# Another fixed order list for a one-core transformer block: loads, evacuations and buffer slots placed anew

## The chip, the cores and the metric

The kernel runs on one core of a Trainium2 chip, in one launch. The metric is device time in microseconds, the median of several runs; lower is better. The core has five instruction queues that run beside each other, each in its own order: TensorE (PE, matrix products into PSUM), VectorE (DVE), ScalarE (ACT), GpSimd (POOL) and the sync queue (SP), which here only issues DMA transfers.

## The reference

One transformer block on x of 2048 tokens by 640, all tensors bf16: memory-augmented attention ("Infini-attention", 32 heads of 20, four segments of 512 tokens), then an MLP of width 1728 with SiLU.

```python
qs, ks, vs = (q[:, :, s].copy(), k[:, :, s].copy(), v[:, :, s].copy())     # s = 0..3
p = _softmax(einsum('bhqd,bhkd->bhqk', qs, ks) * scale + mask)             # causal in the segment
a_dot = einsum('bhqk,bhkd->bhqd', p, vs)
num = einsum('bhld,bhde->bhle', phi(qs), M)
den = einsum('bhld,bhd->bhl', phi(qs), z)[..., None] + 1e-06
o = g * num / den + (1.0 - g) * a_dot
M = M + einsum('bhld,bhle->bhde', phi(ks), vs);  z = z + phi(ks).sum(l)
...
h = x + attention(layernorm(x)) @ wo
out = h + silu(layernorm(h) @ w1) @ w2
```

phi(t) is t + 1 where t > 0 and exp(t) elsewhere.

## The kernel before

The 16 blocks of 128 tokens belong to four segments ("seg 0" to "seg 3") of four blocks. Each segment passes the same stages, and the work of neighbouring segments is interleaved:

- LayerNorm of each block (`n1_st`, `n1_ra`, `n1_rb`, `n1_ap`; lines 711 to 732): statistics on DVE, reciprocal root on POOL in two steps, scaling on DVE. The transposed copy xT is made for the first four blocks by TensorE (`n1_tp`, line 741) and an evacuation on ScalarE (`n1_te`, line 750), for later blocks by a DMA transpose (`n1_tr`, line 756).
- V for one block (`v00` is seg 0, block 0; line 783) with an evacuation (`ve`, lines 793 and 794), and ten projections per segment (`pr`, line 817: `pr` segment, group of heads, 0 for Q or 1 for K) with evacuations (`qe`, lines 825 and 826). Q and K use weights rearranged on chip from wq and wk (`re_`, lines 682 and 684).
- The features phi (`ex`, `pha`, `phb`), copies by DMA that move head parts to other partitions (`vt`, line 857).
- Scores by groups of four heads (`qk`, line 893), their exponentials on ScalarE (`e`, line 904), causal masks on POOL (`mk`, line 915), the product with V (`av`, line 936), its evacuation (`oe`, lines 949 and 951), the transposition and the memory term (`tn`, lines 965 and 969), the normalization on DVE (`nm`) and the sum on POOL (`ad`).
- The memory M (`kt`, `mz`, `ma`, `mb`; line 1058) for the next segment.
- The projection by wo (`ot`, `wo`, line 1119) with the residual (`rs`), a second LayerNorm (`n2_`), the MLP's first product (`h1`, lines 1148 and 1153) with tanh on ScalarE (`th`, line 1162) and a product on DVE into sT (`s`, line 1168), and the second product (`h2`, line 1195), the last residual (`o`, line 1208) and the store (`out`, line 1213).

Nothing is planned at run time or by a cost model. `ORDER` is a list of task names, written out in the kernel. A task is emitted when its name comes up, so the order on every engine's queue, the SP queue's DMAs included, is that of the list. After a name, `/A` or `/D` says whether ScalarE or DVE does an evacuation that both could do, and the numbers after a colon are the buffer slots (PSUM banks, score buffers and so on) that the task's new tiles take. `fill30:0` stands for 30 matmuls on zeros into PSUM bank 0 (line 604), whose result nobody reads. A tracker then adds a semaphore wait wherever an instruction reads what another engine or DMA wrote, or overwrites what another reads.

The loads of weights and of x (lines 567 and 570) are issued by SP, except x2 and x3, which ScalarE issues. `load_x(8, 4)` and `x4` bring four blocks each, `x0` to `x3` one. w1 has five parts by rows (`w_w1_0` to `w_w1_4`), w2 four (`w_w2_0` to `w_w2_3`) and two small ones. wq and wk land in the space of sT and are rearranged from there. `zf0` (ScalarE, line 633) and `zf1` (DVE, line 635) prepare a table from beta; the products `mzc` on POOL (line 657) read it, and `lsc0` to `lsc3` (lines 622 to 630) prepare the scales that `oe` reads. `mt`, `mta`, `mtb` and `mm` are constant masks made on POOL (lines 643 to 653).

Of the kernel before, what the change touches and what calls it, by code (L numbers as in the profile page):

```python
# [6 lines left out]
ALU = mybir.AluOpType  # L7
# [317 lines left out]
D = 640  # L325
# [33 lines left out]
zpad:0 vpad0 iota x3:4 x1:3 x0:7 x2:5 sel w_wv:0 warm:0 vpad1 w_q:0 w_k halfc epsc beta x4:0,1,2,6 n1_st0:1 w_wo:0  # L359
w_w2_4 n1_st1:6 n1_ra0 w_w1_0:0 n1_rb0 n1_ap0:0 n1_ra1 n1_st2:2 fill30:0 n1_tp0:4 n1_rb1 n1_te0/A:0 n1_st3:0 n1_ra2  # L360
epsg0 n1_rb2 fill8:1 v00:0 mt1 n1_ap2:1 n1_ra3 n1_ap1:0 n1_rb3 n1_tp1:2 n1_tp2:6 mt2 n1_ap3:2 n1_te1/A re_wq1/D:0
n1_tp3:4 n1_te2/A re_wq4/D v01:2 ve00/D:1 n1_te3/A re_wq2/A pr010:6 re_wk0/A:0 re_wk1/D ve01/D pr011:7 qe010/D:0
re_wk3/D re_wk4/A lsc0 lsc1 re_wq0/D pr001:0 re_wk2/D qe011/A qk1x0:4 qe001/D:0 pr000:1 e1x2:5 n1_st6:0 e1x0 pr021:0
re_wq3/D qe000/A n1_ra6 mk1x_0 lsc2 n1_st7:4 ex001:0 qk0x0:4 n1_rb6 pr020:2 e0x2:0 mt3 mk1x_256 qe021/D:0 e0x0 lsc3
pr041:3 n1_st5:5 qe020/A vt00:0 n1_st4:7 qk2x0:4 n1_ra5 qe041/A:0 mk0x_0 pr031:1 zf0 vt09 vt06 e2x2:2 n1_rb5 mk0x_256
pr030:0 e2x0 n1_ap5:2 pha041:1 x8:8,9,10,11 qe031/A:0 mk2x_0 vt03 qk0yb0:4 qe030/D av1x:3 e0yb0:1 pr040:2 mk2x_256
n1_ra7 pha001:0 e0yb2 oe1x/D:0 av0x:3 qe040/D mk0yb_0 qk1yb0:4 oe0x/A:1 av2x:0 e1yb0:3 tn1x:1 v03:2 pha021:2 nm1x:3,0
e1yb2 mk0yb_256 phb001 n1_ap6:1 oe2x/A:0 mk1yb_0 qk3x0:4 ve03/D v02:0 n1_tr5:0 vt011 vt07 e3x2:4 vt04 n1_rb7 n1_st9:1
e3x0 ex021:2 ve02/D vt05 vt010 qk4x0:4 mk3x_0 n1_ra4 tn0x:2 e4x0:6 nm0x:0 vt01 mk3x_256 e4x2 n1_st8:6 fill7:3 qk0ya0:0
mta1 vt02 av3x:4 e0ya0:5 mk4x_0 vt08 oe3x/D:1 n1_st10:0 mk4x_256 e0ya2 fill6:5 qk1ya0:4 n1_tr6 v11:0 n1_rb4 e1ya0:0  # L370
n1_st11:3 n1_ra10 mta3 kt00:1 n1_ra8 e1ya2 av4x:2 ve11/D:0 tn2x:3 n1_ra11 phb021 qk5x0:4 n1_ap4:3 fill10:0 v12:0 e5x2:2
n1_ap7:1 n1_tr4 oe4x/D:0 e5x0 nm2x:1 ex011:2 n1_tr7 ve12/D qk6x0:4 mk5x_0 tn4x:2 e6x0:4 av0y:3 nm4x:0 mk5x_256 tn3x:0
e6x2 oe0y/D:0 kt02:0 n1_rb11 av5x:1 ex041:1 n1_ap11:3 qk7x0:4 mk6x_0 v10:2 nm3x:1 w_w2_5 e7x2:6 oe5x/D:1 mta2 mtb3 e7x0
mk6x_256 w_w1_1 w_w1_4 ve10/D qk2ya0:4 mk7x_0 v13:0 e2ya2:5 n1_ra9 mk7x_256 mk1yb_256 e2ya0 tn0y:2 av7x:3 ve13/D n1_rb8
oe7x/A:0 qk2yb0:4 nm0y:1 tn7x:0 e2yb0:1 av6x:1 nm7x:2 tn5x:2 av1y:3 e2yb2 oe6x/D:1 nm5x:3 tn6x:0 oe1y/A:0 qk3ya0:4
mk2yb_0 nm6x:0 e3ya0:2 n1_rb10 ot1:0 mk2yb_256 pha011:0 phb011 e3ya2 tn1y:2 pr101:1 mz02:0 qe101/D:0 av2y:3 ot0 ma02/A:3
qk3yb0:4 oe2y/D:1 mz00:1 e3yb2:0 phb041 pr100:3 ma00/D:0 kt01:1 nm1y:1 e3yb0 tn2y:2 zf1 qe100/D qk4ya0:4 mk3yb_0 kt04:0
wo1:0 e4ya0:6 nm2y:2 mk3yb_256 mtb1 e4ya2 w_w2_2 av3y:3 rs1 w_w1_3 ex031:0 qk4yb0:4 oe3y/D:0 w_w1_2 wo0:0 e4yb2:5
n2_st1:5 w_w2_1 e4yb0 epsg1 tn3y:2 ex101:1 n2_ra1 rs0 mm5 qk5ya0:4 pr140:3 n2_rb1 mk4yb_0 n2_st0:2 e5ya2:0 e5ya0 pr121:0
n2_ap1:0 n2_ra0 nm3y:0 qe140/A:0 mt0 n2_rb0 n2_tr1:0 qk5yb0:4 pr141:1 mta0 e5yb2:3 n2_ap0:2 mk4yb_256 n2_tr0 e5yb0 mtb0  # L380
pha031:1 phb031 av4y:2 mm6 qk6ya0:4 mm4 qe121/D:0 ex140:2 mk5yb_0 pr111:3 e6ya2:6 mk5yb_256 e6ya0 pr120:0 qe111/D:0
qe141/D ex121:0 qk6yb0:4 pha101:2 av5y:3 e6yb0:4 oe4y/D:0 h1_0_7_0:1 qe120/D e6yb2 h1_0_0_0:2 oe5y/D:1 th0_7_0:1 mk6yb_0
mk6yb_256 qk7ya0:4 th0_0_0:0 s0_7_0:0 tn4y:0 h1_0_8_0:3 e7ya0:2 nm4y:3 mz01:1 s0_0_0 mz04:0 e7ya2 ma01/D:2 phb101 kt10:0
kt03:1 h1_0_3_0:2 ma04/D:1 tn5y:1 th0_8_0:1 qk7yb0:4 th0_3_0:0 s0_8_0 av6y:0 e7yb0:0 s0_3_0 h1_0_1_0:3 nm5y:1 e7yb2
h1_0_12_0:2 th0_1_0:1 mk7yb_0 qk8a0:4 th0_12_0:0 pr110:1 e8a2:1 s0_12_0 s0_1_0 mm0 mk7yb_256 e8a0 mzc0 h1_0_10_0:2
qe110/D av7y:3 th0_10_0:1 vt19:0 qk8e0:4 s0_10_0 pr130:1 e8e2:0 vt16 oe6y/D:1 w_w2_3 n1_ap10:2 oe7y/D:0 e8e0 h1_0_5_0:2
pha121:0 qe130/D:0 w_w2_0 h1_0_11_0:3 th0_5_0:1 mk8e_0 qk8b0:4 s0_5_0 th0_11_0:0 tn7y:0 h1_0_6_0:1 e8b0:6 nm7y:3 mz03:2
ma03/D:4 s0_11_0 e8b2 h1_0_2_0:0 pha100:0 n1_ap8:1 h1_0_13_0:2 pha120:0 th0_2_0:1 qk9a0:4 mk8b_0 th0_13_0:0 pr131:3
s0_13_0 e9a2:4 mk8a_0 s0_2_0 mk8b_384 e9a0 h1_0_4_0:0 qe131/D n1_tr8:0 mk8e_256 h1_0_9_0:2 pha141:2 th0_6_0:1 mm3
th0_4_0:0 qk9b0:4 s0_6_0 mzc4 mzc6 ex100:1 mk9a_0 vt17 av8:3 s0_4_0 th0_9_0:1 mzc3 pha110:0 e9b2:3 h2_0_0:0 mm2 phb100  # L390
phb121 s0_9_0 mm9 pha111:1 mtb2 vt18 vt110 mzc9 mm8 e9b0 mm11 h2_0_1 oe8/D:0 mzc5 n1_tr10 ex141:1 mk9b_0 mm10 qk10a0:4
tn6y:3 h2_0_2 e10a2:5 phb141 mm1 vt11 nm6y:0 mzc2 n1_rb9 h2_0_3 e10a0 vt13 mb01:0 mm7 vt111 mzc1 qk10b0:4 mk9b_384 o0
h2_1_0:2 e10b2:2 ot3 mb00:0 e10b0 tn8:0 h2_1_1 n1_tr11 ex120:0 mk10b_0 nm8:2,1 qk10e0:4 ex111:1 h2_1_2 vt15 mk10b_384
phb111 n1_ap9:0 e10e2:1 mk10a_0 vt14 av9:0 e10e0 phb120 ot2 h2_1_3 oe9/A:0 ex110:0 mk10e_0 mk10e_256 qk11a0:4 kt12:1 o1
# [66 lines left out]
def build(nc, es, A_x, A_wq, A_wk, A_wv, A_wo, A_beta, B_x, B_w1, B_w2, out):  # L461
# [52 lines left out]
    zpad = sb("zpad", [128, 256], BF16)  # L514
# [54 lines left out]
    def load_w(k, dst, src, prio, bw, wr, kind="plain", engs=(SP,)):  # L569
# [17 lines left out]
        reads=R((C, ["zpad"])), writes=R((W["w2"], [4, 5]))), [(C, ["zpad"])], [(W["w2"], [4, 5])], -100)  # L587
# [681 lines left out]
```

## Time and profile before

| What | Value |
|---|---|
| median of three runs | 304.64 us (304.49 to 305.93) |
| span of the profiled execution | 303.6 us |
| median less that span | 1.04 us |
| TensorE busy | 294.4 us, 97% |
| DVE, ScalarE, POOL busy | 214.4 (71%), 226.6 (75%), 141.7 us (47%) |
| read from HBM, written | 10.41 MB, 2.62 MB |
| first product with a weight (v00, line 783) starts | 9.03 us |

The profiled execution is known by its span, from the first to the last instruction; the time of a run holds about a microsecond more. PE in the profile is TensorE's matmuls, PEld its weight loads, which run beside them. A row of the timeline or of a group gives line, engine, operation, destination and source, the count, and after the count in brackets how long the engine was idle just before and what ended that. The chain follows the work that ended last backwards to what released it. SPq is the time that SP spends on issuing. In the rows by stage the columns are the window, its length, the busy time of PE, PEld, DVE, ACT and POOL with instruction counts, the granted TensorE clock as a share of full speed, the mean busy share of the 16 DMA engines, and GB/s moved. In the rows on DMA the last number is the median time in us from issue to landing.

### The profile page before, as it was taken

The page shows a single profiled execution, that of the slowest core. Times are in us where ns is not written, and L with a number is a line of the kernel's source. Part 1 is how long each engine was busy: PE and PEld are TensorE (multiplying, and loading weights), DVE is VectorE, ACT ScalarE, POOL GpSimd, SP SyncE. Part 2 cuts the span into 40 slices and gives each one's busy share as a digit, 9 for nine tenths or more (in the row PEclk, how much of TensorE's full clock was granted, in tenths as well). Part 3 has the DMA queues.
Part 4 walks back from the last instruction along what each step waited for, and adds up shares of the span by engine and source line. Part 5 has one row for each costly group of instructions (what it writes and reads, how often), then busy time and mean ns, then how long its engine had stood idle before and what let it go on. Part 6 is the DMA issues. An engine that isn't in the chain of part 4 may idle for free.

```text
span 303.6 us, 7334 instructions
## 1 busy us (share of the span) xinstructions
PE 294.4 (97%) x2934; PEld 167.9 (55%) x2934; DVE 214.4 (71%) x492; ACT 226.6 (75%) x321; POOL 141.7 (47%) x280
## 2 busy tenths in 40 slices
PE   6999989999999999999999999999999999999996
PEld 5634545466565455566643545556564466764565
DVE  4888967877868866958588975858847494835623
ACT  3689988999999999899889989968779951004500
POOL 3346574532875856546847317564564730400000
PEclk9999999999999999999999999999999999999999
DMA  6938375843544130063551300043241006221003
GB/s 211 363 104 159 69 153 87 272 37 77 166 87 75 39 42 2 2 122 69 106 154 42 67 19 0 2 89 69 56 97 36 2 0 89 43 66 66 0 3 107
DMA packets 48721, 24.65 MB, mean 81 GB/s; under 512 B 39152, under 2 KB 47600, under 8 KB 48688
## 3 DMA queue, kind: packets, MB, share of 16 engines
q1 hardware_dynamic: 48400, 23.86, 34.6%
q8 instruction: 23, 0.38, 0.5%
q10 hardware_dynamic: 288, 0.33, 0.4%
q14 instruction: 10, 0.08, 0.1%
HBM read 10.41 MB, written 2.62 MB: 43 GB/s over the span
## 4 chain that ended last, share of the span: by engine, by line
PE 72%; ACT 12%; DVE 7%; DMA 4%; SPq 2%; issue 1%; POOL 0%; ACTq 0%
PE ps_all L1195 17%; PE ps_all L1153 13%; PE ps_all L817 13%; ACT PT L904 8%; PE ps_all L893 7%; PE ps_all L1119 6%; PE ps_all L783 5%; PE ps_all L936 5%; DVE sT L1168 3%; DMA wv_sb<-in_A_wv_dram 2%; ACT th L1162 2%; PE ps_all L965 2%; PE ps_all L1058 2%; DMA x_tok<-in_A_x_dram 1%; PE ps_all L969 1%
## 5 line engine op out<-in xcount | busy, mean ns | idle before, releaser
L904 ACT ACTIVATE PT<-ps_all 128x1024 bf16<-128x1024 f32 (+1 forms) x168 | 156.3, 985 | 16.9 <-PE ps_all L893 15.9
L915 POOL TENSOR_SCALAR_AFFINE_SELECT PT<-PT 128x512 bf16<-128x512 bf16 x128 | 81.5, 650 | 52.8 <-ACT PT L904 51.5
L1195 PE MATMUL ps_all<-w_sb,sT 128*128 128x320 bf16 (+2 forms) x462 | 64.8, 295 | 0.1
L1153 PE MATMUL ps_all<-hT,w_sb 128*128 128x512 bf16 (+1 forms) x325 | 62.5, 337 | 0.5 <-DVE sT L1168 0.4
L1162 ACT ACTIVATE th<-ps_all 128x512 f32<-128x512 f32 (+2 forms) x70 | 34.0, 505 | 35.1 <-PE ps_all L1153 24.6
L1168 DVE SCALAR_TENSOR_TENSOR sT<-th,ps_all 128x512 bf16<-128x512 f32 (+2 forms) x70 | 37.6, 558 | 23.8 <-ACT th L1162 23.2
L1195 PEld LDWEIGHTS ps_all<-w_sb,sT 128*128 128x128 bf16 x462 | 43.2, 98 | 18.5 <-issue 1.9
L1153 PEld LDWEIGHTS ps_all<-hT,w_sb 128*128 128x128 bf16 x325 | 29.8, 98 | 25.4 <-issue 2.1
L1010 POOL TENSOR_TENSOR otok<-on 128x320 bf16<-128x320 bf16 x24 | 19.2, 804 | 23.7 <-DVE on L1002 23.6
L711 DVE BATCH_NORM_STATS2 stt<-x_tok 128x6 f32<-128x320 bf16 x64 | 27.8, 476 | 3.4 <-DMA x_tok<-in_A_x_dram 3.2
L1208 DVE SCALAR_TENSOR_TENSOR x_tok<-ps_all,x_tok 128x640 bf16<-128x640 f32 (+3 forms) x18 | 13.3, 748 | 19.0 <-PE ps_all L1195 18.9
L720 POOL TENSOR_TENSOR rst<-mvt,eps_c 128x1 f32<-128x1 f32 x32 | 7.1, 223 | 40.4 <-DVE mvt L714 36.0
L817 PE MATMUL ps_all<-xT,wqr 128*128 128x512 bf16 x100 | 25.0, 381 | 0.0
L783 PE MATMUL ps_all<-wv_sb,xT 128*128 128x320 bf16 x160 | 24.4, 300 | 0.4 <-DMA wv_sb<-in_A_wv_dram 0.3
L817 PE MATMUL ps_all<-xT,wkr 128*128 128x512 bf16 x100 | 24.8, 380 | 0.0
L1119 PE MATMUL ps_all<-wo_sb,oT 128*128 128x320 bf16 x160 | 24.1, 299 | 0.4 <-DVE rd L996 0.2
L936 PE MATMUL ps_all<-PT,Vx 128*32 128x256 bf16 (+3 forms) x576 | 24.4, 287 | 0.0
L893 PE MATMUL ps_all<-QK 20*128 20x256 bf16 (+3 forms) x360 | 20.5, 286 | 1.0 <-ACT PT L904 0.7
L1002 DVE TENSOR_TENSOR on<-ps_all,rd 128x640 bf16<-128x640 f32 x24 | 19.8, 824 | 1.9 <-POOL otok L1010 1.1
L826 DVE CAST QK<-ps_all 128x512 bf16<-128x512 f32 x25 | 16.9, 684 | 5.1 <-PE ps_all L817 5.0
L1119 PEld LDWEIGHTS ps_all<-wo_sb,oT 128*128 128x128 bf16 x160 | 14.8, 97 | 8.1 <-issue 2.8
L783 PEld LDWEIGHTS ps_all<-wv_sb,xT 128*128 128x128 bf16 x160 | 14.7, 98 | 7.9 <-issue 1.5
(71 smaller groups left out, 329.4 us busy)
## 6 DMA issues: line engine op xcount, KB each, us to landing
out_dram<-x_tok SPq DMA_DIRECT2D x15, 160.0 KB, 1.9
w_sb<-in_B_w_dram SPq DMA_DIRECT2D x5, 432.0 KB, 4.5
x_tok<-in_A_x_dram SPq DMA_DIRECT2D x3, 640.0 KB, 5.3
w_sb<-in_B_w_dram SPq DMA_DIRECT2D x3, 480.0 KB, 3.8
QKV<-QK SPq DMA_DIRECT2D x16, 72.0 KB
wv_sb<-in_A_wv_dram SPq DMA_DIRECT2D x1, 800.0 KB, 7.2
sT<-in_A_wq_dram SPq DMA_DIRECT2D x1, 800.0 KB, 8.9
sT<-in_A_wk_dram SPq DMA_DIRECT2D x1, 800.0 KB, 10.6
```

The lines of the kernel that those rows point to most:

```text
L711: T.add(DV, lambda e, hh=hh: e.bn_stats(out=stt[:, s, 6 * hh:6 * hh + 6], in_=xb[:, 320 * hh:320 * hh + 320]), reads=R((xa, xsub)), writes ...
L783: fns.append(lambda e, c=c, hh=hh: e.matmul(bank(ps, hh)[:, 0:320], lhsT=xT[:, c, 128 * i:128 * i + 128], rhs=wv_sb[:, c, 320 * hh:320 * h ...
L817: fns = [lambda e, kc=kc: e.matmul(bank(ps)[:, lo:hi], lhsT=wt[:, kc, c, :], rhs=xT[:, kc, lo:hi], start=(kc == 0), stop=(kc == NC - 1)) f ...
L893: fns.append(lambda e, j=j, o=o, r=r, q0=q0, q1=q1, qa=qa, ka=ka: e.matmul(ps_all[:, o:o + q1 - q0], lhsT=ka[32 * r:32 * r + DH, 128 * j:1 ...
L904: T.add(AC, lambda e: e.activation(out=pt[:, pta.slot, q0:q0 + 2, 0:width], in_=sc3[:, b0:b0 + 2, 0:width], func=ACT.Exp, scale=SCALE), re ...
L915: T.add(PO, lambda e: e.affine_select(out=v, in_=v, pattern=[[0, 4], [1, 128]], compare_op=ALU.is_ge, fill=0.0, base=0, channel_multiplier ...
L936: fns.append(lambda e, j=j, r=r, h=h, pa=pa, pt=pt, co=co, q0=q0, ji=ji: e.matmul(bank(po)[32 * r:32 * r + 32, q0:hi], lhsT=Vx[:, vx.slot, ...
L1119: fns.append(lambda e, c=c, hh=hh: e.matmul(bank(ps, hh)[:, 0:320], lhsT=oT[:, c, 128 * i:128 * i + 128], rhs=wo_sb[:, c, 320 * hh:320 * h ...
L1153: fns = [lambda e, c=c: e.matmul(bank(ps)[:, lo:hi], lhsT=w1_sb[:, c, 128 * f:128 * f + 128], rhs=hT[:, c, lo:hi], start=(c == 0), stop=(c ...
L1162: T.add(AC, lambda e: e.activation(out=th[:, tha.slot, lo:hi], in_=bank(ps)[:, lo:hi], func=ACT.Tanh, scale=0.5), reads=R((ps, [0])), writ ...
L1168: T.add(DV, lambda e: e.scalar_tensor_tensor(out=sT[:, f, lo:hi], in0=th[:, tha.slot, lo:hi], scalar=1.0, in1=bank(ps)[:, lo:hi], op0=ALU. ...
L1195: fns.append(lambda e, f=f, t0=t0, fr=fr, hh=hh, n=n: e.matmul(bank(pa, hh)[:, 0:n], lhsT=sT[:, f, t0:t0 + 128], rhs=w2_sb[:, fr, c0 + 320 ...
```

## The change

The list holds the same tasks in another order. The tasks' code is the same but for one line. The engine of some evacuations changes, as do most slots. The fillers were 30, 8, 7, 6 and 10 matmuls at five places; they are 44, 19 and 4 at three places, all ahead of the first product with a weight. All loads of the start change places: before, SP issues x1, x0, wv, wq, wk, beta, x4, wo; after, parts of w1 and w2, wo, x8 and beta stand first, wq is the eighth, x0 and x1 come behind it, and wk and wv further down (14th and 17th). The constants on POOL, before spread among the attention of seg 0 and later, stand near the top.

Beside the list, the product into sT is now declared to write two keys in segments 1 to 3, where it declared one; seg 0 has its own two halves as before. The tracker therefore lets these writes also wait for seg 0's readers of the second half.

```diff
 ORDER = """
-zpad:0 vpad0 iota x3:4 x1:3 x0:7 x2:5 sel w_wv:0 warm:0 vpad1 w_q:0 w_k halfc epsc beta x4:0,1,2,6 n1_st0:1 w_wo:0
-w_w2_4 n1_st1:6 n1_ra0 w_w1_0:0 n1_rb0 n1_ap0:0 n1_ra1 n1_st2:2 fill30:0 n1_tp0:4 n1_rb1 n1_te0/A:0 n1_st3:0 n1_ra2
-epsg0 n1_rb2 fill8:1 v00:0 mt1 n1_ap2:1 n1_ra3 n1_ap1:0 n1_rb3 n1_tp1:2 n1_tp2:6 mt2 n1_ap3:2 n1_te1/A re_wq1/D:0
-n1_tp3:4 n1_te2/A re_wq4/D v01:2 ve00/D:1 n1_te3/A re_wq2/A pr010:6 re_wk0/A:0 re_wk1/D ve01/D pr011:7 qe010/D:0
-re_wk3/D re_wk4/A lsc0 lsc1 re_wq0/D pr001:0 re_wk2/D qe011/A qk1x0:4 qe001/D:0 pr000:1 e1x2:5 n1_st6:0 e1x0 pr021:0
...
-e3x0 ex021:2 ve02/D vt05 vt010 qk4x0:4 mk3x_0 n1_ra4 tn0x:2 e4x0:6 nm0x:0 vt01 mk3x_256 e4x2 n1_st8:6 fill7:3 qk0ya0:0
-mta1 vt02 av3x:4 e0ya0:5 mk4x_0 vt08 oe3x/D:1 n1_st10:0 mk4x_256 e0ya2 fill6:5 qk1ya0:4 n1_tr6 v11:0 n1_rb4 e1ya0:0
-n1_st11:3 n1_ra10 mta3 kt00:1 n1_ra8 e1ya2 av4x:2 ve11/D:0 tn2x:3 n1_ra11 phb021 qk5x0:4 n1_ap4:3 fill10:0 v12:0 e5x2:2
...
+w_w1_1:0 mt0:0 w_w2_2:0 x2:5 mt3 zpad mta3 mtb3 w_wo:0 halfc x3:4 iota sel mt2 mta2 mta0 mtb2 x8:8,9,10,11 beta w_w2_1
+w_w1_2 w_q:0 mtb0 mm8 x0:7 epsc n1_st3:0 n1_st0:1 n1_ra3 n1_rb3 warm w_w2_4 n1_ra0 n1_rb0 x1:3 n1_st1:6 n1_ra1 w_w2_0
+epsg0 n1_rb1 mt1 mta1 n1_ap3:2 n1_ap0:0 n1_st2:2 n1_ra2 n1_rb2 n1_ap1:1 n1_st9:1 n1_ap2:3 n1_ra9 mm6 mm9 w_w1_3 n1_rb9
+mm2 mtb1 n1_st10:0 vpad1 w_k w_w2_3 w_w1_4 mm5 mm3 mm0 re_wq1/D:0 re_wq0/D re_wq2/D n1_st8:6 mm11 n1_ra10 n1_rb10
+fill44:0 fill19:1 n1_tp0:6 n1_te0/A:0 w_wv:0 x4:0,1,2,6 fill4:2 n1_tp3:1 n1_te3/A n1_tp1:3 n1_te1/A mm10 v00:6
+ve00/A:1 n1_tp2:2 n1_te2/A re_wq3/A zf0 zf1 re_wk1/D:0 mzc5 mzc11 mzc8 mm4 mzc0 n1_ap10:2 mzc4 re_wk0/D n1_st6:0 mzc6
+lsc0 mm1 mzc2 mm7 lsc1 re_wk2/D mzc3 lsc2 lsc3 n1_ra8 n1_ra6 mzc7 epsg1 n1_st5:5 re_wk4/A mzc1 v01:4 w_w1_0 pr000:0
+pr010:7 n1_ra5 n1_rb5 pr011:1 n1_st4:7 pr001:3 mzc10 n1_rb6 qe010/A:0 ve01/A qe011/A qk1x0:4 pha011:0 n1_rb8 mzc9
...
@@ e_s, the product into sT
-                        op0=ALU.add, op1=ALU.mult), reads=R((ps, [0]), (tha, [0])), writes=R((sa, [(f, q)])))
+                        op0=ALU.add, op1=ALU.mult), reads=R((ps, [0]), (tha, [0])), writes=R((sa, [(f, q)] if s == 0 else [(f, 0), (f, 1)])))
```

In the profile of the changed kernel every line behind the list has a number two higher.

## The prediction

> **What bounds the kernel now.** I read the busy shares first, then the chain that ended last, then the busy times by stage, and last the first 18 us on the sync queue and on TensorE, where the change moves most.
>
> ```profile
> span 303.6 us, 7334 instructions
> PE 294.4 (97%) x2934; PEld 167.9 (55%) x2934; DVE 214.4 (71%) x492; ACT 226.6 (75%) x321; POOL 141.7 (47%) x280
> PE 72%; ACT 12%; DVE 7%; DMA 4%; SPq 2%; issue 1%; POOL 0%; ACTq 0%
> ```
>
> TensorE is busy for 97% of the span and holds 72% of the chain. A list can gain only what TensorE still loses, and it loses whatever delays TensorE's first real work. The stages, as columns of time, then busy time of PE, weight loads, DVE, ACT and POOL:
>
> ```profile
> 9.00:28.00 19.00, 18.90 (x161) 9.26 (x161) 16.12 (x52) 15.35 (x30) 8.46 (x20) 1.00 0.73 215
> 28.00:45.00 17.00, 15.37 (x197) 8.98 (x195) 13.24 (x35) 15.01 (x22) 11.29 (x25) 1.00 0.56 97
> 45.00:80.00 35.00, 34.17 (x418) 19.31 (x419) 28.41 (x78) 33.26 (x51) 15.37 (x35) 1.00 0.56 138
> 80.00:130.00 50.00, 49.06 (x560) 27.46 (x558) 37.90 (x82) 47.30 (x65) 33.71 (x67) 1.00 0.26 45
> ```
>
> After 9 us TensorE idles 0.10, 1.63, 0.83 and 0.94 us in these stages; the later stages to the last matmul add 0.8, so 4.3 us in all. To that come 3.0 us of filler matmuls (line 604: 0.93, 0.83 and 1.26 us at 30.5, 32.1 and 36.1). So 7.3 us is all that a denser body could give back.
>
> Now the start: what the sync queue issues, and when each load landed after its issue.
>
> ```profile
> 1.74 0.44 SPq L570 DMA_DIRECT2D wv_sb<-in_A_wv_dram  x1
> 2.22 0.53 SPq L570 DMA_DIRECT2D sT<-in_A_wq_dram  x1
> 2.79 1.34 SPq L570 DMA_DIRECT2D sT<-in_A_wk_dram  x1
> 4.17 1.84 SPq L579 DMA_DIRECT2D beta_bc<-in_A_beta_dram  x1
> 6.05 0.68 SPq L567 DMA_DIRECT2D x_tok<-in_A_x_dram  x1
> ```
>
> ```profile
> wv_sb<-in_A_wv_dram SPq DMA_DIRECT2D x1, 800.0 KB, 7.2
> sT<-in_A_wq_dram SPq DMA_DIRECT2D x1, 800.0 KB, 8.9
> sT<-in_A_wk_dram SPq DMA_DIRECT2D x1, 800.0 KB, 10.6
> x_tok<-in_A_x_dram SPq DMA_DIRECT2D x1, 640.0 KB, 9.2
> beta_bc<-in_A_beta_dram SPq DMA_DIRECT2D x1, 8.0 KB, 9.4
> ```
>
> The 8 KB of beta take 9.4 us: they landed at 13.6, right behind wk (2.79 + 10.6 = 13.4). The loads of one queue land in the order of their issue, as fast as the bytes ahead of them move. TensorE's first real work, v00 (line 783), starts at 9.03, when wv has landed (1.74 + 7.2 = 8.94):
>
> ```profile
> 1.12 5.03 PE L604 MATMUL ps_all<-zpad 128*128 128x256 bf16 x30 [1.12 <-DVE zpad L583]
> 7.65 1.04 PE L604 MATMUL ps_all<-zpad 128*128 128x256 bf16 x8
> 9.03 1.52 PE L783 MATMUL ps_all<-wv_sb,xT 128*128 128x320 bf16 x10 [0.35 <-DMA wv_sb<-in_A_wv_dram]
> 10.39 1.17 PE L741 MATMUL ps_all<-ident,xn_rot 128*128 128x128 bf16 x15
> ```
>
> **Part 1: the loads change places on the sync queue.** Before, x1 and x0, then wv, wq, wk, beta, x4. After: w1_1, w2_2, wo, x8, beta, w2_1, w1_2, wq, x0, w2_4, x1, w2_0, w1_3, wk, w2_3, w1_4, and only then wv, x4 and w1_0; x2 and x3 stay on ScalarE's queue. Bytes up to and with a load (128 partitions, bf16; w1 0.442 MB, w2 0.492 or 0.655, the square weights 0.819, four blocks of x 0.655, x2 and x3 0.328): wq 4.50 MB, x0 4.66, x1 4.91, wk 6.82, wv 8.58, x4 9.23. Before: wv 1.47 MB, wq 2.29, wk 3.11, x4 3.78.
>
> How far the bytes are when a load lands comes from the rates per microsecond of the trace: 2.08 MB had moved by 9.0 us, and the rows from 9 to 15 us run at 389, 380, 360, 352, 364 and 366 GB/s. Then wv landed with 2.06 MB moved, wq with 2.89, wk with 3.70, x4 with 4.37: each 0.58 to 0.60 MB behind its own place. So wv now lands when 8.58 + 0.59 = 9.17 MB have moved. With 2.08 MB by 9.0 and 368 GB/s (mean of the six rows), that is 9.0 + 7.09/0.368 = 28.3 us. Ends: 404 GB/s (rows from 56 to 60 us, where w1 and w2 come in alone) gives 26.5; 332 GB/s (the row of 15 to 16 us, the slowest with all engines busy) gives 30.4. Most of the bytes are rows of 1,280 B as in the six rows, so I stay near them and take 28.1. The same sum gives x0 17.6, x1 18.3, wk 23.5, x4 30.0.
>
> v00 starts at 28.1 instead of 9.03: **+19.1 us**, all of it before any attention, projection or MLP matmul. On TensorE's list only 67 fillers and the transposes of three blocks stand ahead of v00. Behind it stands the whole rest, which TensorE does at 97% already; nothing there covers the delay.
>
> **Part 2: what is done while TensorE waits.** Three of the four transposes now stand before v00; of 15 matmuls behind it (1.17 us) five are left (0.45): **-0.7**. LayerNorm of x0 to x3 hides under the wait: x1 lands at 18.3, and two statistics tasks (0.9 + 0.2 each), POOL's two steps (0.2 + 0.55), the scaling (0.45) and transposes with their evacuations (0.45 + 0.7) finish by about 23. The masks and tables on POOL (lines 643 to 657 of before, among the attention until 101 us) stand there too and leave POOL freer later; POOL is 47% busy, so I cost this at nothing.
>
> **Part 3: the first stage behind wv.** From v00 to the first score exponential took 16.72 - 9.03 = 7.7 us. After, v00 (1.5), tp2 (0.45), v01 (1.5), four projections (4 x 1.08) and the last evacuation (0.6 and a start of 0.2) give 8.5 us, with one projection more done: no cost. Here is the tightest wait: DVE's zf1 (line 635 of before) waits for zf0, which ScalarE does only behind the evacuations of v00 and of tp2 and a copy of wq: about 28.1 + 1.5 + 0.7 + 0.7 + 0.4 + 0.2 = 31.6. Behind zf1 wait DVE's copies of wk (done by 32.5), the statistics of x4 to x7 (x4 landed at 30.0), and on POOL the products of line 657 (0.2 each) and lsc1. TensorE needs the wk copies at 33.7: hidden. If that cover is gone, each microsecond there is one of the span.
>
> **Part 4: the fillers.** Three groups amid seg 0 (3.0 us) go. The chain runs through ScalarE there:
>
> ```profile
> 28.55 1.51 ACT PT L904 x2
> 30.06 0.52 ACT ex L832
> 30.57 5.12 ACT PT L904 x6
> ```
>
> so TensorE would mostly have idled instead. Bounds 0 and -3.0; I take **-1.0**, nearer the end that this chain gives. The 63 fillers at the start (the first 30 took 5.03, the others would run at 1.26 for ten: 9.2 us) end at about 10 and delay nothing.
>
> **Part 5: a cold start.** The first 30 fillers took 5.03 us; at the pace of the later ten (1.26 us, of which about 0.16 is the tail of the last) they would have taken 3.45. A burst from rest thus costs 1.6 us, although the granted clock reads 1.00 there. In the body no gap is over about 1 us, and none shows such a cost. After the change TensorE rests from about 23 to 28 us. Bounds 0 and +1.6; I take **+1.6**, as the rest before the first burst is the nearer row. The Trainium skill ("TensorE: Matmul & The Clock Gate", Part 1: The HAM clock gate) says that the array runs at half clock until about 3.4 us of work, and falls back after an idle window of about as long; by that rule the sum keeps the 1.6, and without it the sum is 322.0. The trace agrees for the first burst; no run here shows a second one.
>
> **Part 6: order, engines and slots of the body.** Work is the same; only the fillers differ (61 against 67). By engine, of seg 2's ten QK evacuations DVE takes eight instead of five, of its V evacuations three instead of none; ScalarE takes more in segs 0 and 3. DVE (71%) and ACT (75%) have room. Gain at most 4.3 us of idle; loss at worst as if the stage of 28 to 45 us (4.6 us of idle and fillers in 17) went on through 45 to 80: +9. TensorE's rows outside that stage are nearer zero: **0**. The in-order SP and POOL queues move with their producers: the transposes of 2.7 us stand where their inputs are made in both lists.
>
> **Part 7: the second key on sT.** Writes of segs 1 to 3 now also wait for the readers of the other half. The MLP matmul that feeds such a write stands on TensorE behind those readers already; the write waits for that matmul in any case: 0, and where that cover is gone, one matmul group (1.1 to 1.9 us).
>
> **The sum.** 303.6 + 19.1 - 0.7 - 1.0 + 1.6 + 0 = 322.6 us of span. The median of the runs is 304.64, so 1.0 lies around the span: **323.6 us**. Its own range, by the ends of landing (-1.6, +2.3), fillers (-2.0, +1.0) and cold start (-1.6), is 318.5 to 327.
>
> **The rivals.**
> A denser body: POOL, DVE and ScalarE did their preparations during the wait, and the idle 4.3 us and the other 2.0 of fillers come back as well: 317.3, and 313 with the faster loads. For it: POOL's tables no longer stand between masks. Against: ScalarE sets that stage, and its work is the same.
> A body with new waits: ScalarE and DVE each serve the chain behind zf0 and x4, and the loss of 28 to 45 us doubles (+4.6) or spreads (+9): 328 to 332. For it: 19 us of delay bring x4, wk and wv to land close together. Against: the cover worked out in part 3.
> Not slower: the queue's loads move side by side and wv does not stand behind what is issued ahead of it. 16 issues ahead of wv at 0.44 to 0.53 us put its issue at 8.3, and 7.2 us more give 15.5; then +6.5 - 0.7 - 3.0 - 4.3 makes 303.1 at best. It decides if wv lands before 9.0 + 0.7 + 3.0 + 4.3 = 17.0. For it: x2 and x3 on ScalarE's queue landed beside the others after 3.1 us. Against: beta's 9.4 us, and by 17.0 some 5 MB can have moved where 9.17 are needed (540 GB/s; no row is over 430).
>
> **How the numbers follow.** Forecast 0.54, denser body 0.22, new waits 0.20, not slower 0.04. The range 315 to 331 leaves out the last, the lower third of the denser body and the upper third of the new waits, 0.18 together. A change of 0.5% (1.5 us, the spread of the three runs) is about what a measurement can tell. Faster 0.03, same 0.01, slower 0.96.
>
> **What would show it.** In the profile after: v00 at 28 us with wv's landing as its releaser; x0 at 17 to 18; beta landing behind x8; TensorE idle in the third slice; the first score exponential at 37 to 39; v00 at some 2.8 us instead of 1.5 if cold. The forecast is wrong if wv lands before 17, or if TensorE's idle time behind v00 is under 2 or over 9 us.

## The result, and the profile after

The changed kernel takes 324.69 us (323.98 to 325.75 in four runs) against 304.62 for the kernel before: a ratio of 1.0654, 95% interval 1.0626 to 1.0682. The forecast was 323.6, range 315 to 331. A run more than 1.5% above the fastest of its kernel counts as slow and is left out of the median; that is one run, of the last kernel with moved statistics. The profiled execution took 323.98 us, its span is 322.3 us, 18.7 more than before. By the medians the change is 20.1 us, where 19.0 was forecast. The 1.4 us between the two differences is spread among executions: this profile is of the fastest of four, whose spans are 322.3 to 324.0 us. No trace says more of it.

The page of the changed kernel: span, busy shares, engines of the chain.

```profile
span 322.3 us, 7338 instructions
PE 297.9 (92%) x2940; PEld 170.3 (53%) x2940; DVE 221.6 (69%) x498; ACT 223.6 (69%) x315; POOL 143.0 (44%) x280
PE 76%; DVE 8%; ACT 5%; SPq 5%; DMA 4%; issue 1%
```

TensorE's busy time is 3.5 us longer, its share falls from 97% to 92%. The rest of the 18.7 us, 15.2 us, is idle time: 12.3 us of it stand ahead of v00 (14.95 us idle against 2.65), and 2.9 us behind it, where the kernel before ran fillers. What the sync queue issues there (start, time to issue), and what landed how long after its issue:

```profile
0.80 0.90 SPq L572 DMA_DIRECT2D w_sb<-in_B_w_dram  x2
1.74 0.49 SPq L572 DMA_DIRECT2D wo_sb<-in_A_wo_dram  x1
...
11.80 1.25 SPq L572 DMA_DIRECT2D sT<-in_A_wk_dram  x1
13.09 3.90 SPq L572 DMA_DIRECT2D w_sb<-in_B_w_dram  x2
17.03 0.44 SPq L572 DMA_DIRECT2D wv_sb<-in_A_wv_dram  x1
```

```profile
sT<-in_A_wk_dram SPq DMA_DIRECT2D x1, 800.0 KB, 10.8
wv_sb<-in_A_wv_dram SPq DMA_DIRECT2D x1, 800.0 KB, 10.1
```

wk landed at 22.6 and wv at 27.1. SP issued wv only at 17.03: the 16 issues ahead of it took 0.4 to 2.2 us each, and the chain goes through them (SPq) to that point and then through wv's transfer. In the row of 10 to 11 us, shown below, the DMA engines moved only 52 GB/s. So both the issuing and the bytes ahead of wv bear on its time, and no run here separates them. TensorE's timeline, with the idle time and its releaser in brackets:

```profile
1.12 9.65 PE L606 MATMUL ps_all<-zpad 128*128 128x256 bf16 x63 [1.12 <-DVE zpad L585]
20.11 0.71 PE L743 MATMUL ps_all<-ident,xn_rot 128*128 128x128 bf16 x5 [9.34 <-DVE xn_rot L734]
20.62 1.06 PE L606 MATMUL ps_all<-zpad 128*128 128x256 bf16 x4
21.47 1.27 PE L743 MATMUL ps_all<-ident,xn_rot 128*128 128x128 bf16 x10
27.28 2.82 PE L785 MATMUL ps_all<-wv_sb,xT 128*128 128x320 bf16 x10 [4.53 <-DMA wv_sb<-in_A_wv_dram]
```

Two rests, of 9.34 us for x0 and of 4.53 us for wv, and v00 starts at 27.28 instead of 9.03 and takes 2.82 us instead of 1.52. The rows by microsecond (the third number from the end is the granted clock) say why it is slow:

```profile
10.00:11.00 1.00, 0.78 (x8) 0.45 (x5) 0.00 (x0) 0.00 (x0) 0.00 (x0) 1.00 0.20 52
...
12.00:13.00 1.00, 0.00 (x0) 0.00 (x0) 0.00 (x0) 0.00 (x0) 0.00 (x0) 1.00 1.09 433
13.00:14.00 1.00, 0.00 (x0) 0.00 (x0) 0.00 (x0) 0.00 (x0) 0.00 (x0) 0.66 1.00 379
14.00:15.00 1.00, 0.00 (x0) 0.00 (x0) 0.00 (x0) 0.00 (x0) 0.00 (x0) 0.50 1.06 396
...
29.00:30.00 1.00, 1.00 (x6) 0.54 (x4) 0.00 (x0) 0.00 (x0) 0.00 (x0) 0.50 0.09 35
30.00:31.00 1.00, 1.00 (x11) 0.85 (x10) 0.00 (x0) 0.86 (x2) 0.00 (x0) 0.81 0.07 16
31.00:32.00 1.00, 1.00 (x9) 0.65 (x8) 0.00 (x0) 1.00 (x4) 0.00 (x0) 1.00 0.00 0
```

The fillers ended at 10.8; the clock began to fall in the row of 13 to 14 us and came back some 3.1 us after v00 began (0.81 in the row of 30 to 31 us is half clock for its first 0.4 us). Behind v00 the stages, shifted by the delay and set against those of before (columns as there):

```profile
28.00:47.00 19.00, 18.62 (x139) 8.68 (x137) 13.51 (x42) 15.96 (x32) 10.90 (x36) 0.94 0.22 48
47.00:64.00 17.00, 13.85 (x200) 7.49 (x204) 14.78 (x36) 14.78 (x20) 9.79 (x16) 1.00 0.31 62
64.00:99.00 35.00, 34.07 (x429) 19.11 (x425) 27.87 (x79) 32.54 (x51) 15.77 (x27) 1.00 0.31 48
99.00:149.00 50.00, 48.43 (x544) 27.35 (x545) 40.59 (x85) 46.90 (x62) 28.75 (x45) 1.00 0.28 54
```

TensorE idles 0.38, 3.15, 0.93 and 1.57 us in them and 1.1 us later: 7.1 us behind v00, without fillers. Before it was 4.3 us idle and 3.0 us of fillers. From v00's start to the end of the span it is 295.0 us, before 294.6. So 18.25 of the 18.7 us is the later start of v00.

### The profile page after: what moved, and what is told of

Read it like the earlier page. It is cut to its first block, busy times and chain, and to the rows that moved or that the text cites. A ratio compares the mean times of both kernels' runs of the same rounds, so it can differ in the third digit from the quotient of the medians.

```text
span 322.3 us, 7338 instructions
## 1 busy us (share of the span) xinstructions
PE 297.9 (92%) x2940; PEld 170.3 (53%) x2940; DVE 221.6 (69%) x498; ACT 223.6 (69%) x315; POOL 143.0 (44%) x280
## 4 chain that ended last, share of the span: by engine, by line
PE 76%; DVE 8%; ACT 5%; SPq 5%; DMA 4%; issue 1%
PE ps_all L1197 19%; PE ps_all L1155 17%; PE ps_all L819 11%; PE ps_all L895 7%; PE ps_all L1121 6%; PE ps_all L938 5%; PE ps_all L785 5%; ACT PT L906 5%; SPq L572 3%; DMA wv_sb<-in_A_wv_dram 3%; PE ps_all L967 2%; PE ps_all L1060 2%; PE ps_all L971 2%; DMA oT<-otok 1%; DVE QK L828 1%; SPq L569 1%
## 5 line engine op out<-in xcount | busy, mean ns | idle before, releaser
L1170 DVE SCALAR_TENSOR_TENSOR sT<-th,ps_all 128x512 bf16<-128x512 f32 (+2 forms) x70 | 37.7, 560 | 18.7 <-ACT th L1164 18.1
L785 PE MATMUL ps_all<-wv_sb,xT 128*128 128x320 bf16 x160 | 25.7, 310 | 6.0 <-DMA wv_sb<-in_A_wv_dram 4.5
L1012 POOL TENSOR_TENSOR otok<-on 128x320 bf16<-128x320 bf16 x24 | 19.2, 800 | 15.2 <-DVE on L1004 15.2
L828 DVE CAST QK<-ps_all 128x512 bf16<-128x512 f32 x28 | 19.1, 684 | 4.5 <-PE ps_all L819 4.2
L834 ACT ACTIVATE ex<-QK 128x512 bf16<-128x512 bf16 x30 | 19.3, 651 | 1.3 <-DVE phiK L847 1.1
## 6 DMA issues: line engine op xcount, KB each, us to landing
sT<-in_A_wk_dram SPq DMA_DIRECT2D x1, 800.0 KB, 10.8
```

Of the source, the lines that this page charges most:

```text
L785: fns.append(lambda e, c=c, hh=hh: e.matmul(bank(ps, hh)[:, 0:320], lhsT=xT[:, c, 128 * i:128 * i + 128], rhs=wv_sb[:, c, 320 * hh:320 * h ...
L1170: T.add(DV, lambda e: e.scalar_tensor_tensor(out=sT[:, f, lo:hi], in0=th[:, tha.slot, lo:hi], scalar=1.0, in1=bank(ps)[:, lo:hi], op0=ALU. ...
```

## The experiments

All ratios are to the kernel before, with 95% intervals. In the diffs a list's entries stand one after the other as in `ORDER`; entries without a mark are there for the place only.

### The late loads alone, on the list of before

```diff
 ORDER (the list of before)
-zpad:0 ... x3:4 x1:3 x0:7 x2:5 ... w_wv:0 ... w_q:0 w_k ... beta x4:0,1,2,6 ... w_wo:0 w_w2_4 ...
+zpad:0 w_w1_1:0 w_w2_2:0 x2:5 w_wo:0 x3:4 x8:8,9,10,11 beta w_w2_1 w_w1_2 w_q:0 x0:7 warm w_w2_4 x1:3 w_w2_0
+w_w1_3 w_k w_w2_3 w_w1_4 w_wv:0 x4:0,1,2,6 w_w1_0 ... (then the list of before, without these)
```

> The list of before, with its loads at the start put into the order that the changed list has (x2 and x3 stay on ScalarE's queue; zpad and the first tanh stand ahead, as one small load waits for them). Theory (the order of the loads carries the whole loss): wv lands at about 27, v00 starts there instead of at 9.03, and the array is cold: 304.6 + 18.2 + 1.4 = 324.2, between 322 and 326. Rival (the body's order carries a good part of it, the loads matter less): 305 to 315.

Measured: 324.96 us, 1.0669 (1.0652 to 1.0685), where the whole change gives 1.0654. In this kernel v00 looks as in the changed one:

```profile
27.94 2.82 PE L785 MATMUL ps_all<-wv_sb,xT 128*128 128x320 bf16 x10 [5.21 <-DMA wv_sb<-in_A_wv_dram]
```

Moving the loads alone costs as much as the whole change: where the loads stand in the list is sufficient for the loss. The next runs ask from the other side.

### One load back, then three, then all that are needed

Three kernels, each the changed list with loads put first on the sync queue:

```diff
 ORDER (the changed list)
+w_wv:0                                                       (first kernel)
+x1:3 x0:7 w_wv:0                                             (second)
+x1:3 x0:7 w_wv:0 w_q:0 w_k beta:0 x4:0,1,2,6 x8:8,9,10,11 w_wo:0   (third)
 w_w1_1:0 mt0 w_w2_2:0 x2:5 mt3 zpad ... (without the entries that were moved up)
```

> The changed list with one load moved: wv first on the sync queue. Theory (each load lands by the bytes ahead of it, and the next late load takes over): x0 lands some 1.5 us later than in the changed kernel because of wv's 0.82 MB, the transposes end at about 23.8 and v00 starts there instead of at 27.3; then wk (24.7) and above all x4 (29.9, unchanged) hold DVE, whose copies and evacuations come 3.4 us earlier than in the changed kernel: 321.2, between 320 and 322.5. Rival (wv alone sets the start, and the end follows v00 one for one down to what x0 allows): the same 3.5 us here, so this run tells the two apart only together with the next. Rival (loads don't queue behind each other): no change, 324.7.

> The changed list with x1, x0 and wv first on the sync queue. Theory (the next late load takes over): v00 starts at 11 to 12, behind the 63 fillers, 15 us earlier than in the changed kernel; but wq lands at 19.6, wk at 24.7 and x4 at 29.9, and DVE, which does the statistics of x4 ahead of its next copies, comes to the evacuation of the third pair of projections only 3.4 us earlier than in the changed kernel: 320.5, between 319 and 322, hardly better than with wv alone first. Rival (the end follows v00): 324.7 less 15 to 16, some 309.

> The changed list with all loads that the first stage needs ahead of the others: x1, x0, wv, wq, wk, beta, x4, x8, then the rest. Nothing else moves. Theory: wv lands at about 9, but DVE does the statistics of x8 to x10 ahead of the last scaling and of the copies of wq; x8 lands at about 16, the copies of wk are done by about 23, and the first four projections end at about 24.7 instead of 36.2: 324.7 - 11.5 = 313.2, between 310 and 316. Rival (the order of the loads is all, DVE's order matters nothing): 305 to 307.

Measured: 320.80 (1.0536, 1.0516 to 1.0557), 321.52 (1.0556, 1.0529 to 1.0583) and 315.06 us (1.0342, 1.0322 to 1.0362). All three lie in their expected ranges, and the second is no better than the first. Wv first brings v00 to 24.90 and the third pair of projections to 32.99 (36.46 in the changed kernel); the span is shorter by as much, 318.8. With x0 and x1 first too, TensorE does v00 at 11.76 and then rests again and again. Its timeline, and DVE's, in the second kernel:

```profile
11.76 1.52 PE L785 MATMUL ps_all<-wv_sb,xT 128*128 128x320 bf16 x10
...
23.38 3.94 PE L819 MATMUL ps_all<-xT,wqr 128*128 128x512 bf16 x10 [3.31 <-DVE wqr L686]
28.05 2.33 PE L819 MATMUL ps_all<-xT,wkr 128*128 128x512 bf16 x10 [0.73 <-DVE wkr L686]
...
33.03 1.84 PE L819 MATMUL ps_all<-xT,wkr 128*128 128x512 bf16 x5 [2.37 <-DVE lsc L629]
```

```profile
22.50 1.06 DVE L686 COPY wqr<-sT 128x400 bf16<-128x400 bf16 x6 [4.76 <-DMA sT<-in_A_wq_dram]
...
27.57 0.42 DVE L686 COPY wkr<-sT 128x400 bf16<-128x400 bf16 x2 [2.94 <-DMA sT<-in_A_wk_dram]
...
31.47 0.89 DVE L713 BATCH_NORM_STATS2 stt<-x_tok 128x6 f32<-128x320 bf16 x2 [2.80 <-DMA x_tok<-in_A_x_dram]
```

v00 is 15.5 us earlier, and the third pair of projections, at 33.03, stands where it stood with wv alone: each late load hands over to the next, wq, wk, x4. The work gained at v00 is only spread between rests, and some of it is done at half clock (the projections of 23.38 take 3.94 us for what takes 2.32 at full). Of the first kernel's expectation one detail fell: DVE was held there not by x4, which had landed when its turn came at 30.3, but by the chain of v00, zf0 and zf1 (zf1 at 29.12).

In the third kernel the loads of seg 0 are early, and DVE's own order is the wait: the statistics of x8 to x10 stand ahead of the last scaling of seg 0. DVE waits 7.63 us for the landing of x8, and TensorE then 5.89 us for the scaling behind it:

```profile
17.63 0.89 DVE L713 BATCH_NORM_STATS2 stt<-x_tok 128x6 f32<-128x320 bf16 x2 [7.63 <-DMA x_tok<-in_A_x_dram]
```

```profile
19.12 0.71 PE L743 MATMUL ps_all<-ident,xn_rot 128*128 128x128 bf16 x5 [5.89 <-DVE xn_rot L734]
```

### The other loads on another queue

```diff
-    load_x(0, 1, -100, 2.30, "fix", (SP,))
+    load_x(0, 1, -100, 2.30, "fix", (AC,))
 ... (the same for x1, wv, wq, wk and x4)
 ORDER (the changed list)
+x2:5 x3:4 x1:3 x0:7 w_wv:0 w_q:0 w_k x4:0,1,2,6
 w_w1_1:0 ... (the rest as it was)
```

> The changed kernel with x1, x0, wv, wq, wk and x4 issued by ScalarE, behind x2 and x3, and the other loads on the sync queue in their order. Nothing else moves. Theory (in one queue loads wait for the bytes ahead, two queues share the engines): each queue moves at about half of 390 GB/s, so x0 and x1 land at 7, wv at 11, wq at 15, wk at 20, x4 at 23; x8, on the sync queue, at 16. DVE reaches the third pair of projections some 11 us earlier than in the changed kernel: 313, between 309 and 318. Rival (the bytes in flight count, whatever the queue): no better than the kernel with wv alone first, 321.

Measured: 318.31 us, 1.0440 (1.0423 to 1.0457): better than with wv first on one queue, and 0.3 us above the expected range of 309 to 318. Landing times, from the issues at 3.30 (wv), 4.53 (wk) and 7.03 (x4):

```profile
wv_sb<-in_A_wv_dram ACTq DMA_DIRECT2D x1, 800.0 KB, 10.4
sT<-in_A_wk_dram ACTq DMA_DIRECT2D x1, 800.0 KB, 19.5
x_tok<-in_A_x_dram ACTq DMA_DIRECT2D x1, 640.0 KB, 20.8
```

wv landed at 13.7 with 1.47 MB of its own queue moved, wk at 24.0 with 3.11, x4 at 27.8 with 3.77, where 11, 20 and 23 were expected. So a second queue does move beside the first; loads wait for the bytes ahead of them in their own queue. But the shares weren't halves: from wv to wk 1.64 MB in 10.3 us, 159 GB/s of some 375 (the mean of 14 to 24 us). The sync queue held rows of 1,280 B and w1's rows of 3,456 B, the other queue rows of 1,280 B alone. The Trainium skill ("DMA: Bandwidth & Descriptors", Queues, rings and completion order) says that each engine takes turns between queues packet by packet; turns of unequal packets would fit, but no run varied the row size, so that is an argument, not shown.

### The cold start

```diff
 ... fill4:2 n1_tp3:1 n1_te3/A n1_tp1:3 n1_te1/A mm10
+fill24:2
 v00:6 ...
```

> The changed kernel with 24 more filler matmuls between the transposes of the first blocks and v00, while TensorE waits for wv: they start cold and should bring the granted clock back to 1.00 before wv lands. Theory (the cold start lies on the path): v00 takes 1.5 us instead of 2.8, and the time falls by 1.3 us, to 323.3. Rival (ScalarE or DVE set the first stage's end): v00 gets shorter, the time stays within 0.4 us. If the fillers don't bring the clock back, neither changes.

Measured: 322.32 us, 1.0569 (1.0551 to 1.0587), against 1.0654 for the changed kernel: 2.4 us less by the medians. Timeline and clock:

```profile
22.88 3.40 PE L606 MATMUL ps_all<-zpad 128*128 128x256 bf16 x24 [0.26 <-ACT xT L752]
27.22 1.53 PE L785 MATMUL ps_all<-wv_sb,xT 128*128 128x320 bf16 x10 [0.94 <-DMA wv_sb<-in_A_wv_dram]
```

```profile
23.00:24.00 1.00, 1.00 (x6) 0.69 (x6) 0.96 (x5) 0.42 (x1) 1.00 (x5) 0.50 1.03 410
24.00:25.00 1.00, 1.00 (x10) 0.86 (x9) 1.00 (x3) 0.00 (x0) 1.00 (x6) 0.92 1.04 389
25.00:26.00 1.00, 1.00 (x11) 0.90 (x10) 1.00 (x5) 0.00 (x0) 0.92 (x5) 1.00 1.06 369
```

v00 takes 1.53 us, the first projections start at 30.23 instead of 31.77, 1.5 us earlier, and the span is 1.6 us shorter. The cold start lay on the path. What the medians show beyond 1.6 lies within the two intervals.

### The fillers of the kernel before

```diff
-... e4x2 n1_st8:6 fill7:3 qk0ya0:0 ... e0ya2 fill6:5 qk1ya0:4 ... n1_ap4:3 fill10:0 v12:0 ...
+... e4x2 n1_st8:6 qk0ya0:0 ... e0ya2 qk1ya0:4 ... n1_ap4:3 v12:0 ...
```

> The kernel of before without its three groups of fillers amid segment 0 (23 matmuls on zeros, whose result nobody reads). Theory (ScalarE's exponentials set that stage, the fillers cover idle time; the prediction took 1.0 us for them): 303.6, between 302 and 304.8. Rival (each filler delays the next score): 301.6. Rival (TensorE's pauses slow its clock): over 305.

Measured: 305.30 us, 1.0013 (0.9996 to 1.0029): no difference. It lies 0.5 us above the expected range, and so by its number where the rival stood that TensorE's pauses slow its clock; but the clock reads 1.00 in every stage, so that rival isn't seen. In the stage of 28 to 45 us TensorE is busy 13.56 us instead of 15.37:

```profile
28.00:45.00 17.00, 13.56 (x196) 7.34 (x192) 14.66 (x38) 15.72 (x22) 11.21 (x25) 1.00 0.50 118
```

The fillers stood in idle time, as the chain through ScalarE said; the prediction's gain of 1.0 us for them was 0.

### Repairing the start of the changed list

Is the body of the changed list, freed of the late loads, worth that of before? Three kernels start from the one with all needed loads first, and move LayerNorm work of x8 to x10 (and x11) out of DVE's way, with the first fillers cut from 63 to 30:

```diff
 (first)   ... n1_ap5:0
+n1_st9:1 n1_ra9 n1_rb9 n1_st10:2 n1_ra10 n1_rb10 n1_st8:6 n1_ra8 n1_rb8 n1_ap10:2
 (second)  ... ve03/D
+n1_st9:1 n1_ra9 n1_rb9
 ... oe0x/D:1
+n1_st10:2 n1_ra10 n1_rb10
 ... oe3x/D:1
+n1_ap10:2 n1_st8:6 n1_ra8 n1_rb8
 ... av4x:6
+n1_ap8:3
 (third)   as the second, and n1_ap0:0 stands ahead of n1_st1:6, and n1_st11:3 n1_ra11 n1_rb11 behind oe4x/D:0
```

> As the kernel with all needed loads first, and three more edits at the start of the changed list: the statistics of x8 to x10 with their root and the scaling of x10 move behind the copies of wk and the first evacuations, and the first fillers are 30 instead of 63. Theory (loads and DVE's waits for them are the whole loss, the body of the changed list is worth the same as that of before): 304.6 to 309; I expect 306, as POOL's 24 small mask operations stand ahead of the scales lsc that DVE waits for at some 18 us. Rival (the body has its own loss of 4 us or more): over 309. Rival (the body is denser once the loads are right): under 303.

> As the kernel with all needed loads first and the statistics of x8 to x10 moved, but these statistics no longer stand in one block ahead of DVE's copies of wk for the fourth projections: they come one block at a time, behind the evacuations of V and of the first attention outputs. Theory (the 3.0 us that TensorE waited for these copies, and the cold start of 2.4 us behind that rest, were the edit's own; the body of the changed list is worth that of before): 309.99 less 4.5 to 5.4, so 305.0, between 304 and 306.5; v00 at about 10.3 where before has 9.0. Rival (the body has a loss of its own): over 307.5.

> The same with the scaling of x0 ahead of the statistics of x1 on DVE, as before has it, and the statistics of x11 moved back as well. Theory: the transposes and v00 start 1 us earlier, near 9.3, and DVE is freer in the first stage: 304.2, between 303 and 305.5, no different from before. Rival (DVE's order in the first 10 us doesn't matter, as wq and wk land at 11 and 13.4): as the run beside it.

Measured: 309.99 (1.0165, 1.0145 to 1.0186), 314.08 (1.0315, 1.0271 to 1.0358) and 314.66 us (1.0254, 1.0200 to 1.0309; its five runs spread from 310.36 to 314.93). The first missed its expected range by 1 us, the others by 7.6 and 9.2. By number the first two lie where their rival stood, that the changed body has a loss of its own. The first has v00 at 10.29 and, behind the block of statistics, this:

```profile
27.88 2.29 PE L819 MATMUL ps_all<-xT,wkr 128*128 128x512 bf16 x5 [3.00 <-DVE wkr L686]
30.10 0.51 PE L895 MATMUL ps_all<-QK 20*128 20x256 bf16 x8
30.54 2.85 PE L785 MATMUL ps_all<-wv_sb,xT 128*128 128x320 bf16 x10
```

3.0 us of rest and 2.4 us of slow matmuls (2.29 and 2.85 us for 1.25 and 1.53). Spread out, the statistics took that rest away and made another, at 40 us, when DVE waited for POOL's root of a block and the next evacuation stood behind it. From the second kernel:

```profile
40.14 2.83 PE L785 MATMUL ps_all<-wv_sb,xT 128*128 128x320 bf16 x10 [2.38 <-DVE oTs L953]
...
45.47 2.87 PE L785 MATMUL ps_all<-wv_sb,xT 128*128 128x320 bf16 x10
```

```profile
38.00:39.00 1.00, 0.00 (x0) 0.00 (x0) 0.15 (x1) 1.00 (x2) 0.69 (x2) 0.99 0.00 0
39.00:40.00 1.00, 0.00 (x0) 0.00 (x0) 0.84 (x3) 0.32 (x1) 0.66 (x2) 0.50 0.00 0
...
48.00:49.00 1.00, 1.00 (x11) 0.27 (x10) 0.97 (x3) 0.07 (x1) 0.65 (x2) 0.50 0.00 0
49.00:50.00 1.00, 1.00 (x8) 0.69 (x7) 0.66 (x1) 1.00 (x2) 0.00 (x0) 0.89 0.00 0
```

The clock stayed at 0.50 for some nine microseconds of TensorE work, from 40.1 to 49.2. My expectation counted the moved statistics by their duration and did not ask which evacuation then stands behind a wait. The third kernel has v00 at 11.27, where 9.3 was expected, and two rests like that one, of 2.40 us at 36.6 (for the DMA transpose of a block) and of 2.70 us at 44.4 (for DVE's oTs); it is no different from the run beside it, as its rival said. Together, the rest and the slow matmuls of the first kernel are about the 5.0 us by which it is slower than before, which would leave little for a loss of the body; that is a sum, not a run. In the other two the rests that the moves made stand in the way of an answer.

### The start of before with the body of the changed list

Two lists run that of before up to an entry and go on with the changed list:

```diff
 (first)   the first 215 entries of the list of before, then the changed list's remaining entries;
           constants, statistics and loads from its top keep their places of before
 (second)  the first 709 entries of the list of before, then the changed list's remaining entries
```

> The list of before up to the place that it reaches at about 42 us (its first 215 entries), then the changed list's order, engines and slots. The constants, small statistics and weight loads that the changed list had put at its top keep their places of before. No slot had to be altered. Theory (the body of the changed list is worth that of before): TensorE idled 2.6 us behind 45 us in before and 3.6 us behind the same point in the changed kernel, so 304.7 + 1.0 = 305.7, between 304 and 308. Rival (the body is denser, and the loads alone hid it): under 303. Rival (the body is worse, as the runs with statistics moved suggest): over 309.

> The list of before up to the place that it reaches at about 118 us (its first 709 entries), then the changed list. No slot had to be altered. Theory (as beside it): TensorE idled 0.8 us behind 130 us in before, 1.1 us behind the same point in the changed kernel, so 305.0, between 304 and 306.5. Rival (denser): under 303.5. Rival (worse): over 307.

Measured: 312.24 us (1.0249, 1.0224 to 1.0275) and 308.95 us (1.0127, 1.0109 to 1.0145): above the expected ranges by 4 and 2.5 us, where the rival of a worse body stood. Both show rests at the seam: in the first 1.75 and 1.17 us at 42 to 43 us, and then half clock (V takes 2.82 us at 44.39). In the second, TensorE's waits behind 112 us are:

```profile
PE ps_all L819 <- DVE on L1004: 1.0, 1, 1.0
PE ps_all L785 <- DVE sT L1170: 0.8, 1, 0.8
PE ps_all L967 <- ACT PT L906: 0.7, 1, 0.7
PE ps_all L1155 <- DVE sT L1170: 0.6, 1, 0.6
```

The first and the third are at the seam (122 and 124 us). The second and the fourth, 1.4 us at 133 and 136 us, are in the changed kernel too, with 0.9 and 0.6 us at the same instructions, and not in before: the changed body has these two waits of its own. No kernel separates the body from its start without a seam, so whether the changed body, with a start made for it, would equal before stays open; by its own trace it loses 7.1 us behind v00 against 7.3 before. No kernel here beats that of before.

## Why the prediction was right

- **Part 1, the loads.** Right, and it carries the result. wv landed at 27.1 (forecast 28.1, ends 26.5 to 30.4), v00 started 18.25 us later (forecast 19.1). wk landed at 22.6 (23.5), and x0's statistics start at 17.27 (17.6). The miss of 1.0 us at wv is made of parts that differ in sign: 2.44 MB had moved by 9.0 us, where 2.08 was reckoned, and wv landed 0.38 MB behind its place in the queue, where 0.59 was taken, while from 9.0 to 27.1 us the engines moved 359 GB/s on the mean, where 368 was taken. The forecast treats the queue as full throughout; the row of 10 to 11 us, at 52 GB/s, shows that it was not. Moving the loads alone, on the list of before, gives the same time.
- **Part 2, work under the wait.** Right: seg 0's statistics, roots and scalings (the last ends at 22.75), three of the five copies of wq and most of the masks on POOL are done by 27 us, and only five transposing matmuls stand behind v00. The other masks and the products mzc come behind zf1, from 32.66 on. The gain of 0.7 us that the prediction booked for the transposes was about 0.5.
- **Part 3, the first stage.** Right: zf1 ran at 32.40, 5.1 us behind v00's start where 3.5 was reckoned; 1.3 of that is the cold v00, which the reckoning left out. The first copies of wk ended at 32.9, and TensorE did not wait for them. The first score exponential came at 36.78, just ahead of the 37 to 39 forecast.
- **Part 4, the fillers.** A term mis-sized: -1.0 was taken, taking them out of the kernel of before gave 0. The end of the range that the ScalarE chain spoke for was the right one.
- **Part 5, the cold start.** Right: 1.6 forecast; v00 takes 1.3 us longer, and with fillers that restore the clock the first projections start 1.5 us earlier and the span is 1.6 shorter. The Trainium skill ("TensorE: Matmul & The Clock Gate", Part 1: The HAM clock gate) gives half clock after an idle window of about 3.4 us and for about 3.4 us of work; here the clock fell within 3.2 us after the fillers and came back 3.1 us after v00 began. But the prediction named the wrong rest: the clock fell in the rest for x0 (10.8 to 20.1 us), not in the one of 23 to 28 us, and the transposes between the two didn't bring it back.
- **Part 6, the body.** Forecast 0, measured -0.2 by idle time and fillers (7.1 against 7.3), the sum of a better stage around seg 0 and 1.3 us more idle later. That engines and slots moved made no difference that the total shows.
- **Part 7, the key on sT.** Right: with and without that edit the changed list gives the same program, instruction by instruction and wait by wait. The further waits that the section on the change speaks of do not arise in this order.
- **The sum.** The span was forecast at 322.6 and is 322.3. What lies around a span was taken as 1.0; the profiled execution has 1.7, and so have all others here. That the span comes out to 0.3 us is in part luck: v00 came 0.85 us earlier than forecast, and the gain of 1.0 us from the fillers did not come. Two small sums of the prediction are off: the lower end of its range adds up to 318.4, not 318.5, and its 313 for faster loads would be 315.7 (317.3 less 1.6), or 314.1 if the cold start goes too.
- **The rivals.** Not slower: out, by beta, wv and wk and by the run with two queues. What it reckoned for SP's issues, 0.44 to 0.53 us each, was short too: 16 of them took until 17.03 us, and lines that the prediction shows already had 1.34 and 1.84. A denser body: not seen. New waits: 1.5 us of them (133 to 136 us in the second seam kernel, and at the same places here), not the 4.6 that the rival needed.

## What to carry to other kernels

Before judging a reordering by its thousand moves, add up the bytes that each queue must move ahead of the first load that the main engine needs: that sum, at the rate of the trace, gave wv's landing here to within 1 us, in part by errors that offset each other, and moving the loads alone reproduced the loss. When one late load is repaired, look for the next one in line on every engine; putting two more loads early gained nothing until all of them were. In a list that keeps TensorE busy, a small task moved within another engine's queue can cost twice, as the rest that it makes and as slow matmuls behind that rest.

## What the runs showed that I had not expected

The clock needs little rest to fall, and can stay low long. In the first kernel with moved statistics a rest of 3.0 us began at 24.9 us; the clock reads 0.79 in the row of 26 to 27 us and 0.50 in the next, so by the mean of its row it fell some 1.7 us into the rest. In the second, after a rest that began at 37.8 us, shortly behind one of half a microsecond, it reads 0.99 in the row of 38 to 39 us and 0.50 in the next: some 1.3 us. In the changed kernel it was some 2.5 us. It came back after 3.1 us from the start of v00 there, after 5.5 us of work in the first kernel with moved statistics, and after nine in the second, where much of the work was small score and attention matmuls. Whether the kind of matmuls decides that is not shown; no run varies it alone. And two DMA queues that were both full did not share evenly: 159 of some 375 GB/s went to the one that held rows of 1,280 B alone.
